# A gated attention and FFN block: the order of every engine fixed in the kernel by a model of engine times

## The chip, the cores and the metric

The kernel runs on one core of one Trainium2 chip. The metric is the device time of one execution in microseconds (us). All runs quoted here are in the fast state (the record calls a run slow when it takes over 1.5% longer than the fastest of the same kernel), and medians are given with the range of the runs. The granted clock is the share of TensorE's full clock that the profile shows as granted. A "ratio" is the mean time of one kernel's fast runs over the mean of the other kernel's fast runs of the same rounds, so it is not quite the ratio of the two medians that stand beside it. The kernel before was timed again in each batch of runs (medians 803.54 to 805.38), and every ratio is taken within its own batch. The kernel after was timed in the first comparison only. So the differences to it in us, given below, are between medians of different batches, and they are uncertain by some 2 us, as the medians of the kernel before show. The three batches of experiments also ran on three different chips.

Engine names in the profile: PE is the matmul engine (TensorE), PEld its weight load, DVE is VectorE, ACT is ScalarE, POOL is GpSimd, and SP issues most of the DMAs. "L182" is line 182 of that kernel's file; the two kernels and the experiments have different line numbers.

## The reference, cut to what matters

```python
x = A_x                                         # 2048 tokens x 1024
g = sigmoid((x * gate_w).sum(-1, keepdims=True))
a = windowed_attention(x @ wqkv) @ wo           # 32 heads, window of 8 keys, dilation 2
b = (gelu(x @ w_gate) * (x @ w_up)) @ w_down    # 1024 -> 3584 -> 1024
return g * a + (1 - g) * b                      # bf16
```

## The kernel before

The tokens are cut into four chunks of 512, numbered c. FFN runs twice, each time over two chunks ("FFN 0" for chunks 0 and 1, "FFN 1" for 2 and 3). Each chunk needs: projections to q, k, v (PE); a gate (PE matmul, then a VectorE transpose `zt`, a clip `zc`, a ScalarE exp `ez`); attention (nearly all VectorE); its share of FFN (PE, with ScalarE and VectorE moving each product out of PSUM, the memory into which PE writes); and the down stage, which multiplies the FFN result by `w_down` and the attention result by `wo` together.

FFN and the down stage use a scheme of seven block products in place of eight. It needs sums and differences of blocks of the operands, called form sums here: of `w_down` and `wo` (prepared once, `prep_forms`), of the FFN weights (in FFN 0), of x and of the FFN result. These form sums are VectorE work too.

Here are the parts that the argument touches:

```python
def gate(c):
    pz = bank("pz")
    for kt in range(KT):
        nc.tensor.matmul(pz[:], lhsT=gcol[:, kt:kt + 1].to_broadcast([P, P]), rhs=xT(c, kt), ...)
    zt = work.tile([P, SC], F32, tag="u2", bufs=2, name="zt")
    nc.vector.transpose(out=zt[:], in_=pz[:])                               # L182
    nc.vector.tensor_scalar(out=zc[:], in0=<column of zt>, ...)             # L184, clip
    nc.scalar.activation(out=ez[:], in_=zc[:], func=ACT.Exp)                # L187
    ...

def prep_forms(i0):
    ...
    nc.vector.tensor_tensor(out=fo[:, 0], in0=b12, in1=b11, op=ALU.subtract)       # L297
    nc.vector.tensor_tensor(out=fo[:, 1], in0=b22, in1=fo[:, 0], op=ALU.subtract)  # L298
    ...                                                                            # L299, L300

def ffn(sup):
    for i in range(FT + 2):                        # FT = 28
        if i < FT:
            A[f] = bank("pA")
            mm(A[f], "A11", B11, f, True)          # L343: the first product
            Bk[f] = bank("pB")
            with hp():
                nc.scalar.copy(out=Bk[f][:], in_=A[f][:])   # L363: the "seed", PE adds onto it
    ...

# main program (hp() marks high priority for the scheduler)
qkv_outer(0, 0, wq)
prep_forms(0); prep_forms(2)
qkv_one(0, 1, wk)
qkv_one(0, 2, wv)
with hp():
    gate(0)
for i0 in range(4, NPREP, 2):
    prep_load(i0)
    prep_forms(i0)
attention(0)
halo(1)
qkv_one(1, 0, wq); qkv_one(1, 1, wk); qkv_one(1, 2, wv)
with hp():
    gate(1)
attention(1)
for sup in range(NSUP):
    c0 = 2 * sup
    x_forms()
    ffn(sup)
    if sup + 1 < NSUP:
        load_xT(c0 + 2)                            # 8 transposing loads of x on SP
    down(c0)
    ...                                            # qkv, gate, attention, load_xT, down of the next chunks
```

The program order gives only priorities. A scheduler in the framework decides, when the kernel is built, in which order each engine gets its instructions. What follows from such an order is shown by the traces below: an engine stands idle for the instruction at the head of its queue while work behind it is ready.

Of the kernel before, what the change touches and what calls it, by code (L numbers as in the profile page):

```python
# [12 lines left out]
AP = bass.AP  # L13
# [10 lines left out]
HP = 100000  # L24
# [3 lines left out]
def _win_ap(src: bass.AP, dims):  # L28
    return AP(src.tensor, src.offset, [list(src.ap[0])] + [list(d) for d in dims])


@with_exitstack
def kernel(
# [38 lines left out]

    consts = ctx.enter_context(tc.tile_pool(name="consts", bufs=1))
    persist = ctx.enter_context(tc.tile_pool(name="persist", bufs=1))
    ring = ctx.enter_context(tc.tile_pool(name="ring", bufs=5))
    work = ctx.enter_context(tc.tile_pool(name="work", bufs=2))
    small = ctx.enter_context(tc.tile_pool(name="small", bufs=1))
    psum = ctx.enter_context(tc.tile_pool(name="psum", bufs=8, space=bass.MemoryType.PSUM))
# [10 lines left out]
    vT = [persist.tile([P, NT, HALO + SC], BF16, name=f"vT{i}") for i in range(2)]  # L89
    gcol = consts.tile([P, KT], BF16)  # L90
    ident = consts.tile([P, P], BF16)

# [6 lines left out]
    def ring_tile():  # L99
        return ring.tile([P, RT], BF16, tag="ring", name="rg")  # L100

    def bank(name):
        return psum.tile([P, SC], F32, tag="mm", name=name)

    def hp():
        return tc.high_priority(offset=HP)

# [4 lines left out]
    pwarm = bank("pwarm")  # L112
    for i in range(5):
        nc.tensor.matmul(pwarm[:], lhsT=warm[:, 0:P], rhs=warm, start=True, stop=True)
# [3 lines left out]
    for i in range(1):  # L118
        nc.vector.memset(kT[0][:, :, 0:HALO], 0.0)
        nc.vector.memset(vT[0][:, :, 0:HALO], 0.0)  # L120

    def qkv_load(which, pieces, vbuf=False):
        tiles = []
        for hf in range(2):
            if vbuf:
                wv = hT[:, hf * KH:(hf + 1) * KH, 0:NT, :].rearrange("p k f n -> p k (f n)")
            else:
                wv = ring_tile()[:].rearrange("p (k n) -> p k n", k=KH)
            for (k0, k1) in pieces:
                r0 = (hf * KH + k0) * P  # L130
                nc.sync.dma_start(out=wv[:, k0:k1, :],
                                  in_=A_wqkv[r0:r0 + (k1 - k0) * P, which * D:(which + 1) * D]
                                  .rearrange("(k p) n -> p k n", p=P))
            tiles.append(wv)
        return tiles

    def qkv_mm(ps, tiles, t, kt, c):
        lhsT = _win_ap(tiles[kt // KH][:, kt % KH, t:t + 1], [[NT, P]])
        nc.tensor.matmul(ps[:], lhsT=lhsT, rhs=xT(c, kt), start=(kt == 0), stop=(kt == KT - 1))  # L139

    def halo(c):
        cc = c % 2
        if c > 0:
            pc = 1 - cc
            nc.scalar.copy(out=kT[cc][:, :, 0:HALO], in_=kT[pc][:, :, SC:SC + HALO])
            nc.scalar.copy(out=vT[cc][:, :, 0:HALO], in_=vT[pc][:, :, SC:SC + HALO])
# [5 lines left out]
    def qkv_outer(c, which, tiles):  # L152
        banks = [bank("ps") for t in range(NT)]
        for kt in range(KT):
            for t in range(NT):
                qkv_mm(banks[t], tiles, t, kt, c)
        for t in range(NT):
            if t % 2 == 0:
                nc.scalar.copy(out=qkv_dst(c, which, t), in_=banks[t][:])
            else:  # L160
                nc.vector.tensor_copy(out=qkv_dst(c, which, t), in_=banks[t][:])

    def qkv_one(c, which, tiles):
        for t in range(NT):
            ps = bank("ps")
            for kt in range(KT):
                qkv_mm(ps, tiles, t, kt, c)
            nc.scalar.copy(out=qkv_dst(c, which, t), in_=ps[:])

    def qkv(c):  # L170
        halo(c)
        for which in range(3):
            qkv_one(c, which, qkv_load(which, [(0, KH)]))

    gates = {}

    def gate(c):
        pz = bank("pz")
        for kt in range(KT):
            nc.tensor.matmul(pz[:], lhsT=gcol[:, kt:kt + 1].to_broadcast([P, P]), rhs=xT(c, kt), start=(kt == 0), stop=(kt == KT - 1))  # L180
        zt = work.tile([P, SC], F32, tag="u2", bufs=2, name="zt")
        nc.vector.transpose(out=zt[:], in_=pz[:])  # L182
        zc = small.tile([P, SC // 32], F32, tag="zc", name="zc")
        nc.vector.tensor_scalar(out=zc[:], in0=zt[:].rearrange("p (b j) -> p b j", j=32)[:, :, 0],  # L184
                                scalar1=ZMAX, scalar2=-ZMAX, op0=ALU.min, op1=ALU.max)
        ez = small.tile([P, SC // 32], F32, tag="ez", bufs=2, name="ez")
        nc.scalar.activation(out=ez[:], in_=zc[:], func=ACT.Exp)  # L187
        og = small.tile([P, SC // 32], F32, tag="og", name="og")
        nc.vector.tensor_scalar(out=og[:], in0=ez[:], scalar1=1.0, scalar2=1.0, op0=ALU.mult, op1=ALU.add)
        nc.vector.reciprocal(out=og[:], in_=og[:])  # L190
        omg = small.tile([P, NST], F32, tag="omg", bufs=3, name="omg")
        for q in range(4):
            nc.vector.tensor_copy(out=omg[32 * q:32 * (q + 1), :],
                                  in_=og[32 * q:32 * (q + 1), :].rearrange("p (j q) -> p j q", q=4)[:, :, q])
        gates[c] = (ez, omg)

    def attention(c):
        cc = c % 2
        q_, k_, v_ = qo[cc], kT[cc], vT[cc]
        ez = gates[c][0]  # L200
        for a in range(SC // AC):
            a0 = a * AC
            acc = work.tile([P, NWIN, AC], BF16, tag="b0", bufs=1, name="acc")
            for t in range(NT):
                q_b = q_[:, t, a0:a0 + AC].rearrange("p (o s) -> p o s", o=1).to_broadcast([P, NWIN, AC])
                k_w = _win_ap(k_[:, t, HALO + a0:HALO + a0 + AC], [[-DIL, NWIN], [1, AC]])
                if t == 0:
                    nc.vector.tensor_tensor(out=acc[:], in0=q_b, in1=k_w, op=ALU.mult)
                else:
                    prod = work.tile([P, NWIN, AC], BF16, tag="b1", bufs=1, name="prod")  # L210
                    nc.vector.tensor_tensor(out=prod[:], in0=q_b, in1=k_w, op=ALU.mult)  # L211
                    nc.vector.tensor_tensor(out=acc[:], in0=acc[:], in1=prod[:], op=ALU.add)  # L212
            accT = work.tile([P, CW, DL], BF16, tag="b1", bufs=1, name="accT")
            nc.vector.transpose(out=accT[:].rearrange("p c d -> p (c d)"), in_=acc[:].rearrange("p w s -> p (w s)"))
            nxt = work.tile([P, CW, 2], BF16, tag="s4", bufs=1, name="nxt")
            nc.vector.tensor_tensor(out=nxt[:], in0=accT[:, :, 0:2], in1=accT[:, :, 2:4], op=ALU.add)
            lsb = work.tile([P, NWIN, CB], F32, tag="b1", bufs=1, name="lsb")
            nc.vector.tensor_tensor(out=lsb[:].rearrange("p w c -> p (w c)"), in0=nxt[:, :, 0], in1=nxt[:, :, 1],
                                    op=ALU.add)
            if c == 0 and a == 0:  # L220
                for q in range(4):
                    for w in range(1, NWIN):
                        nc.vector.memset(lsb[32 * q:32 * q + DIL * w, w, 0:HQ], NEG)
            m4 = small.tile([P, 4, CB], F32, tag="m4", name="m4")
            nc.vector.tensor_tensor(out=m4[:], in0=lsb[:, 0:4, :], in1=lsb[:, 4:8, :], op=ALU.max)
            nc.vector.tensor_tensor(out=m4[:, 0:2, :], in0=m4[:, 0:2, :], in1=m4[:, 2:4, :], op=ALU.max)
            nc.vector.tensor_tensor(out=m4[:, 0, :], in0=m4[:, 0, :], in1=m4[:, 1, :], op=ALU.max)
            m_b = m4[:, 0:1, :].to_broadcast([P, NWIN, CB])
            nc.vector.tensor_tensor(out=lsb[:], in0=lsb[:], in1=m_b, op=ALU.subtract)
            nc.scalar.activation(out=lsb[:], in_=lsb[:], func=ACT.Exp, scale=scale)  # L230
            d4 = small.tile([P, 4, CB], F32, tag="m4", name="d4")
            nc.vector.tensor_tensor(out=d4[:], in0=lsb[:, 0:4, :], in1=lsb[:, 4:8, :], op=ALU.add)
            nc.vector.tensor_tensor(out=d4[:, 0:2, :], in0=d4[:, 0:2, :], in1=d4[:, 2:4, :], op=ALU.add)
# [12 lines left out]
            for t in range(0, NT, 2):  # L246
                pall = work.tile([P, 2, NWIN, AC], BF16, tag="b0", bufs=1, name="pall")
                for u in range(2):
                    v_w = _win_ap(v_[:, t + u, HALO + a0:HALO + a0 + AC], [[-DIL, NWIN], [1, AC]])
                    nc.vector.tensor_tensor(out=pall[:, u], in0=ab[:], in1=v_w, op=ALU.mult)  # L250
# [147 lines left out]
    def down(c):  # L398
# [21 lines left out]
        def quarter(j, kh):  # L420
            return (hq(j, kh), oq(j, kh))
# [194 lines left out]
```

## Time and profile before

| | before |
|---|---|
| device time, median (range) | 805.86 us (804.89 to 805.9), 3 of the 4 runs of the result below |
| span of the profiled run, granted clock | 802.9 us, 0.972 |
| matmuls of 512 columns in the program | 3376 |
| their pitch (from the start of one to the start of the next) at full clock | 4 in 0.863 us, so 0.2158 us each: 729 us |
| start before the first projection, tail after the last product | 8 and 4 us (the prediction booked 5) |
| floor from these | 740 us (742 in the prediction) |

The pitch agrees with the Trainium skill, "TensorE: Matmul & The Clock Gate", Part 1, which gives 215.7 ns. The first lines below are from the profile page of the kernel before: the busy table, three rows of the picture in 40 slices (a digit is the busy share of a slice in tenths; one slice is 20 us; PEclk is the granted clock in tenths) and the chain of work that ended last, as shares of the span.

```profile
PE 743.0 (93%) x3345; PEld 370.6 (46%) x3413; DVE 599.7 (75%) x811; ACT 302.6 (38%) x511; POOL 48.4 (6%) x81
...
PE   8992967999999995999999999599989999999998
...
DVE  2457999988999895999989989979989533631201
...
PEclk9996997999999997999999999799999999999999
...
PE 58%; DVE 22%; DMA 8%; issue 5%; ACT 3%; SPq 1%; POOL 1%; ACTq 0%; DVEq 0%; POOLq 0%
```

PE is the limit nearly everywhere, with dips in four places: around 60 to 80, 110, 305 and 510 us. In each the granted clock drops as well. PE's own waits, the three largest (total, times, longest, in us), name the dips:

```profile
PE pA L343 <- ACT pB L363: 20.3, 5, 9.7
PE ps L139 <- DVE zt L182: 14.2, 1, 14.2
PE qA L466 <- DMA rg<-in_B_w_down_dram: 9.2, 2, 8.6
```

The 14.2 us is the gate of chunk 0, at 63 to 78 us. The 20.3 us are seeds before FFN 0 (9.4) and FFN 1 (9.7) and three short ones. The 8.6 us is a wait at 307 us for down weights: in SP's timeline transposing loads of x stand ahead of them.

What kept `zt` away for so long stands in VectorE's timeline (start, duration, instruction, and in brackets the idle time before it and what ended that):

```profile
61.17 0.69 DVE L297 TENSOR_TENSOR hT<-hT 128x1024 bf16<-128x1024 bf16 x1 [2.35 <-DMA hT<-in_B_w_down_dram]
...
66.98 0.69 DVE L299 TENSOR_TENSOR hT<-hT 128x1024 bf16<-128x1024 bf16 x1 [1.58 <-DMA hT<-in_B_w_down_dram]
...
72.51 0.69 DVE L299 TENSOR_TENSOR hT<-hT 128x1024 bf16<-128x1024 bf16 x1 [1.89 <-DMA hT<-in_A_wo_dram]
...
74.91 0.69 DVE L297 TENSOR_TENSOR hT<-hT 128x1024 bf16<-128x1024 bf16 x1 [1.10 <-DMA hT<-in_A_wo_dram]
...
76.12 1.22 DVE L211 TENSOR_TENSOR prod<-qo_81,kT_83 128x2048 bf16<-128x2048 bf16 x1
77.25 0.71 DVE L182 STREAM_TRANSPOSE zt<-pz 128x512 f32<-128x512 f32 x1
```

The gate matmul had ended at 52 us. VectorE came to `zt` at 77.25, because preparation sums that waited for their loads stood before it in the queue. VectorE was idle for each of them, while attention work of chunk 0 stood behind it. Summed over the run, the first line below (from the groups: busy us, mean ns, then idle time just before the group and what ended it) has 21.8 us of such idleness. The second is from the windows view and has the busy time of VectorE and PE from 20 to 120 us:

```profile
L297 DVE TENSOR_TENSOR hT<-hT 128x1024 bf16<-128x1024 bf16 x9 | 6.2, 691 | 21.8 <-DMA hT<-in_B_w_down_dram 20.7 <-DMA hT<-in_A_wo_dram 1.1
```

Gate 1 is late. Its matmul ended at 111.6 us, and `zt` follows ten attention steps of chunk 0; these are the last step and `zt`:

```profile
120.40 1.22 DVE L250 TENSOR_TENSOR pall<-ab,vT_85 128x2048 bf16<-128x2048 bf16 x1
121.53 0.71 DVE L182 STREAM_TRANSPOSE zt<-pz 128x512 f32<-128x512 f32 x1
```

### The profile page before, as it was taken

Reading aid. Unit: us, or ns where it says so; the run is one execution under the profiler, and the core shown is the slowest. Engines: PE = TensorE matmul, PEld = TensorE weight load, DVE = VectorE, ACT = ScalarE, POOL = GpSimd, SP = SyncE. Lnnn points to the kernel's source line nnn. Section 1 sums busy time; section 2 is a strip of 40 time slices with the busy share of each in tenths; the row PEclk is TensorE's granted clock in tenths of the full one; section 3 lists DMA queues with packets and bytes.
Section 4 is the critical chain, followed back from the end, with each engine's and each line's share of the span. In section 5 each row is a group of like instructions: output and inputs, shape, how many; then the busy total and the mean of one; then the engine's idle time right before and its main releaser. Section 6 shows DMA issues by size and latency. Waiting matters only on the chain.

```text
span 802.9 us, 9027 instructions
## 1 busy us (share of the span) xinstructions
PE 743.0 (93%) x3345; PEld 370.6 (46%) x3413; DVE 599.7 (75%) x811; ACT 302.6 (38%) x511; POOL 48.4 (6%) x81
## 2 busy tenths in 40 slices
PE   8992967999999995999999999599989999999998
PEld 5661643444444442446654466244434444444443
DVE  2457999988999895999989989979989533631201
ACT  1320244566545740113331043275575555310110
POOL 2144100000000000010000000000000000001000
PEclk9996997999999997999999999799999999999999
DMA  9999530546546379897558973325444454789984
GB/s 309 308 343 375 165 124 2 180 142 202 163 152 210 106 228 235 292 313 255 169 183 295 325 267 107 93 91 169 133 158 145 131 182 146 235 290 324 324 316 174
DMA packets 128523, 167.84 MB, mean 209 GB/s; under 512 B 17888, under 2 KB 105952, under 8 KB 124896
## 3 DMA queue, kind: packets, MB, share of 16 engines
q1 hardware_dynamic: 122112, 139.48, 54.0%
q0 software_dynamic: 6080, 27.27, 8.8%
q8 instruction: 26, 0.43, 0.2%
q10 hardware_dynamic: 288, 0.52, 0.2%
q14 instruction: 17, 0.14, 0.1%
HBM read 135.79 MB, written 28.31 MB: 204 GB/s over the span
## 4 chain that ended last, share of the span: by engine, by line
PE 58%; DVE 22%; DMA 8%; issue 5%; ACT 3%; SPq 1%; POOL 1%; ACTq 0%; DVEq 0%; POOLq 0%
PE ps L139 12%; PE qB L466 10%; PE pB L343 9%; PE qD L466 8%; PE qA L466 8%; PE pA L343 6%; PE pD L343 6%; DVE acc L212 3%; DVE prod L211 3%; DVE pall L250 2%; DMA hT<-in_B_w_down_dram 2%; DMA rg<-in_A_wqkv_dram 2%; DMA rg<-in_B_w_down_dram 2%; DVE hT L382 2%; DVE hT L369 2%
## 5 line engine op out<-in xcount | busy, mean ns | idle before, releaser
L343 PEld LDWEIGHTS <-rg 128*128 128x128 bf16 x1568 | 154.3, 98 | 215.6 <-issue 35.1
L139 PE MATMUL ps<-xr,rg 128*128 128x512 bf16 x626 | 140.9, 383 | 16.7 <-DVE zt L182 14.2
L343 PE MATMUL pA<-xr,rg 128*128 128x512 bf16 x439 | 115.3, 383 | 21.0 <-ACT pB L363 20.3
L139 PEld LDWEIGHTS <-rg 128*128 128x128 bf16 x640 | 91.9, 144 | 65.0 <-issue 17.2
L343 PE MATMUL pB<-tf,rg 128*128 128x512 bf16 x439 | 115.4, 383 | 1.7 <-DVE hT L382 0.8
L466 PEld LDWEIGHTS <-hT 128*128 128x128 bf16 x672 | 66.1, 99 | 90.4 <-DMA rg<-in_B_w_down_dram 9.1
L466 PE MATMUL qB<-rg,hT 128*128 128x512 bf16 x330 | 76.1, 379 | 0.3
L212 DVE TENSOR_TENSOR acc<-acc,prod 128x2048 bf16<-128x2048 bf16 x56 | 68.3, 1220 | 1.0
L466 PE MATMUL qA<-rg,hT 128*128 128x512 bf16 x220 | 53.3, 390 | 9.4 <-DMA rg<-in_B_w_down_dram 9.2
L343 PE MATMUL pD<-xr,rg 128*128 128x512 bf16 x220 | 57.8, 383 | 3.0 <-ACT m_4599 L377 1.3
L343 PE MATMUL pB<-xr,rg 128*128 128x512 bf16 x218 | 56.8, 379 | 0.4 <-ACT u_2264 L392 0.2
L343 PE MATMUL pD<-tf,rg 128*128 128x512 bf16 x220 | 57.0, 379 | 0.2
L369 DVE TENSOR_TENSOR hT<-hT,gl 128x1024 bf16<-128x1024 bf16 x56 | 38.3, 684 | 18.0 <-ACT hT L368 17.8
L388 ACT ACTIVATE gl<-pA 128x512 bf16<-128x512 f32 x56 | 33.5, 599 | 30.6 <-PE pA L343 27.1
L363 ACT COPY pB<-pA 128x512 f32<-128x512 f32 x56 | 32.3, 576 | 30.8 <-PE pA L343 30.8
L470 POOL DMA_DIRECT2D out_dram<-ost x24 | 13.0, 542 | 448.9 <-ACT ost L492 341.1
L250 DVE TENSOR_TENSOR pall<-ab,vT_86 128x2048 bf16<-128x2048 bf16 x32 | 38.7, 1216 | 0.0
L250 DVE TENSOR_TENSOR pall<-ab,vT_85 128x2048 bf16<-128x2048 bf16 x32 | 38.6, 1217 | 0.0
L211 DVE TENSOR_TENSOR prod<-qo_81,kT_83 128x2048 bf16<-128x2048 bf16 x28 | 34.2, 1222 | 1.1
L211 DVE TENSOR_TENSOR prod<-qo_82,kT_84 128x2048 bf16<-128x2048 bf16 x28 | 34.1, 1219 | 0.8
L368 ACT CAST hT<-pB 128x512 bf16<-128x512 f32 x56 | 32.2, 575 | 5.2 <-PE pB L343 4.8
L510 DVE SCALAR_TENSOR_TENSOR ost<-qB,omg,m5d 128x512 bf16<-128x512 f32 x8 | 6.0, 747 | 35.0 <-issue 28.7
(548 smaller groups left out, 841.8 us busy)
## 6 DMA issues: line engine op xcount, KB each, us to landing
rg<-dforms SPq DMA_DIRECT2D x32, 896.0 KB, 6.6
rg<-in_B_w_down_dram SPq DMA_DIRECT2D x24, 896.0 KB, 6.7
rg<-in_A_wqkv_dram SPq DMA_DIRECT2D x14, 1024.0 KB, 7.9
rg<-in_B_w_gate_dram SPq DMA_DIRECT2D x28, 512.0 KB, 3.9
fforms<-rg POOLq DMA_DIRECT2D x14, 1024.0 KB, 6.4
rg<-fforms SPq DMA_DIRECT2D x14, 1024.0 KB, 4.8
rg<-oforms SPq DMA_DIRECT2D x16, 512.0 KB, 3.5
hT<-in_B_w_down_dram SPq DMA_DIRECT2D x28, 256.0 KB, 6.6
```

The source lines that it names most:

```text
L139: nc.tensor.matmul(ps[:], lhsT=lhsT, rhs=xT(c, kt), start=(kt == 0), stop=(kt == KT - 1))
L211: nc.vector.tensor_tensor(out=prod[:], in0=q_b, in1=k_w, op=ALU.mult)
L212: nc.vector.tensor_tensor(out=acc[:], in0=acc[:], in1=prod[:], op=ALU.add)
L250: nc.vector.tensor_tensor(out=pall[:, u], in0=ab[:], in1=v_w, op=ALU.mult)
L343: nc.tensor.matmul(bk[:], lhsT=w, rhs=rhs[:, k, :], start=(start and k == 0), stop=(k == KH - 1), skip_group_check=True)
L363: nc.scalar.copy(out=Bk[f][:], in_=A[f][:])
L368: nc.scalar.copy(out=hs(f, 0), in_=v3(Bk[f][:]))
L369: nc.vector.tensor_tensor(out=hT[:, :, f, :], in0=hT[:, :, f, :], in1=gl[f][:].rearrange("p (j s) -> p j s", s=P), op=ALU.mult)
L382: nc.vector.tensor_tensor(out=hs(f, 1), in0=v3(Bk[f][:]), in1=v3(m5[f][:]), op=ALU.add)
L388: nc.scalar.activation(out=gl[f][:, SC:2 * SC], in_=A[f][:], func=ACT.Gelu_apprx_tanh)
L466: nc.tensor.matmul(bk[:], lhsT=l, rhs=w[i], start=(start and i == 0), stop=(i == n - 1), skip_group_check=True)
L470: eng.dma_start(out=o2[s0 + j * P:s0 + (j + 1) * P, nh * NW:(nh + 1) * NW], in_=ost)
```

## The change

Its intent: don't leave the order to the scheduler. Every operation becomes an `Op` with an engine, a modelled cost and the operations that it needs. Six streams (the matmul stages, loads, weight form sums, x form sums, preparation sums, attention) are Python generators. At each step the stream whose next operation can start earliest by the model (plus a small fixed bias of its stream) gets its turn. Each instruction is then chained to the one before it on its engine, so that the scheduler can't move it. Buffers (PSUM banks, the ring of weight slots, attention's scratch) are handed out by the same model.

```diff
+class Weave:
+    def _start(self, op):
+        ...
+        t = self.clk[op.eng]
+        for d in deps:
+            t = max(t, d.end + self.LAT + (op.lag if d.eng != op.eng else 0.0))
+        return t
+
+    def _emit(self, op, t):
+        ...                                     # advance the engine's modelled clock, call op.fn()
+            prev = self.last.get(eng)
+            if prev is not None:
+                self.tc.add_manual_dep(ins, prev, ..., reason="engine order")
+            self.last[eng] = ins.name
+
+    def run(self, streams):
+        while live:
+            ...                                 # the stream with the smallest t + bias goes next
+            self._emit(s[2], t)
@@
+    MM = 0.2128                                 # modelled us of one matmul
@@
+    def tt(n, f32=False):                       # modelled us of a VectorE tensor_tensor
+        return 0.07 + n / (960.0 if f32 else 1920.0)
@@ the transposing loads of x go two by two behind down weights
-        if sup + 1 < NSUP:
-            load_xT(c0 + 2)
-        down(c0)
+        yield from load_down(c0, load_x(c0 + 2, [("ffn", sup)]) if more else ())
@@ the gate
-        with hp():
-            gate(0)
+        e = dve(0.63, lambda: nc.vector.transpose(out=zt[:], in_=banks[i][:]), [o])
+        ...
+        e = act(0.1, lambda: nc.scalar.activation(out=ez[:], in_=zc[:], func=ACT.Exp), [e], table="exp", lag=1.0, ...)
@@ end of the program
+    w.run([(0.0, main()), (0.0, loads()), (0.1, wforms()), (0.1, x_forms()), (0.15, preps()), (0.3, attention())])
... (the bodies of ffn, down, attention and the loads are rewritten as generators; the expansion copy
     `ex` and the transpose behind it in attention are cut into halves; the arithmetic stays)
```

The matmuls are the same, and so is nearly all VectorE and ScalarE work.

## The prediction

> **What bounds it now.** TensorE. The table of engines has it 93% busy, but the floor is its pitch: in the timeline 4 FFN matmuls of 512 columns take 0.863 us, 0.2158 each (the Trainium skill, "TensorE: Matmul & The Clock Gate", Part 1, gives 215.7 ns warm; the trace agrees). The kernel has 3376: 729 us. With 8 us before the first projection and 5 after the last: about 742. The span is 802.9, so some 60 us are stalls. The list of PE's waits and the timeline place them:
> - 63-78 us: 14.2 us on the VectorE transpose of gate(0), which stood behind attention and form sums waiting for loads;
> - 114-124 and 507-517: 9.4 and 9.7 us before FFN 0 and FFN 1. The releaser shown is a ScalarE seed, but in the chain of waits that stood behind VectorE's gate transpose (121.5, 514.5), again behind attention;
> - 306-315: 8.6 us for the first down weights, queued on SP behind 16 transposing loads of x.
> A granted clock of 0.5-0.7 follows each, some 2 us more (the same page says an idle array falls to half clock). The rest: table loads in FFN 1 (2 us), and FFN iterations of 6.2 us where 28 matmuls need 6.04.
>
> **What changes.** Same matmuls, almost the same VectorE and ScalarE work (ex and its transpose are halved: 2 us less blocking). Order, fixed buffers and the SP queue change. From the built order: gate transposes stand where their matmul should end; the form sums of x come before gate(0); weight forms of block 0 before the last preparation loads; down weights before the x transposes, which go two by two into the down stage.
>
> **Budget.** I summed the measured VectorE pitches (2048 elements 1.14 us, 1.26 when it reads what the one before wrote; 1024: 0.60; PSUM operand 0.62; transpose 2.22) along the new order. Gate(1) falls at 95 us, as in PE's own count, so FFN 0 should start at 98-101 rather than 124. In FFN 0 VectorE needs 5.94 us per iteration, PE 6.04: nearly a tie, and as gelu stands before the next seed on ScalarE, PE follows VectorE with little slack. I take 6.2, as before: end about 273. Down(0), projections, down(1), projections: 54.4+43+54.4+43 us, plus 3 for each down stage (its DMA share is already 0.86-0.92, and 8 x transposes come on top): 474. From gate(2) to gate(3) VectorE needs about 103 us against PE's 97.5: 3 us of stall before FFN 1. FFN 1 172, down(2) and down(3) 109, tail 5: span about 762, device time 764.
>
> So 33 us of gate stalls, 9 of the down start and 5 of cold clock lie on the critical path and go; some 10 come back as coupling of PE to VectorE and DMA pressure.
>
> **Prediction:** 764 us, 8 in 10 between 751 and 784. Faster by over 2%: 0.92; within 2%: 0.06; slower: 0.02.
>
> **What would show it.** PE's waits on gate transposes and seeds under 3 us each; FFN 0 starting at 98-101; no gap at the first down stage; granted clock above 0.98 on average; FFN iterations 6.1-6.3 us, with short PE waits on ScalarE seeds released through VectorE; down(0), down(1) 54-58 us at a DMA share over 0.9.
>
> **What would make it wrong.** The order comes from a model whose VectorE ops are cheaper (1.14, never 1.26): if VectorE lags, an in-order ScalarE hands each lag to PE, and FFN iterations grow to 6.5 us (+16). Late preparation loads could stop VectorE before gate(0). Transposing loads could starve down weights by over 5 us per stage. Better: FFN iterations at 6.04, then 752.

## More of the kernel before

VectorE is under-used in the first four slices and then close to full until about 640 us.

```profile
20.00:120.00 100.00, 78.36 (x349) 49.85 (x355) 72.14 (x123) 26.95 (x49) 24.34 (x34) 0.92 0.81 264
```

The columns of a window are: bounds and length; busy time and count of PE, PEld, DVE, ACT and POOL; granted clock, DMA share, GB/s. VectorE worked 72.14 of these 100 us and PE 78.36.

## The result and the profile after

| | before | after |
|---|---|---|
| device time, median (range), 4 runs each | 805.38 us (803.16 to 805.9) | 766.98 us (766.42 to 767.78) |
| ratio of fast runs, 95% interval | | 0.9529, 0.9509 to 0.9549 |
| span of the profiled run | 802.9 us | 764.6 us |
| granted clock | 0.972 | 0.990 |

The page of the kernel after, the same rows:

```profile
PE 738.1 (97%) x3345; PEld 370.3 (48%) x3413; DVE 606.3 (79%) x827; ACT 303.4 (40%) x519; POOL 48.3 (6%) x81
...
PE   8999989999999999999799997999999999999997
...
DVE  2799999999999799989999989989998933603201
...
PEclk9999999999999999999899999899999999999999
...
PE 79%; DVE 10%; DMA 5%; ACT 4%; issue 2%; SPq 0%; ACTq 0%; DVEq 0%
```

Busy time hardly moved on any engine (VectorE even has 6.6 us more). What went is PE's idleness: the dips at 60 to 80, 110 and 305 us are gone, smaller ones are left at 375 and 480 us. VectorE is nearly full from the second slice on. PE's largest waits are now:

```profile
PE ps_90 L656 <- ACT ps_94 L683: 6.3, 1, 6.3
PE ps_94 L801 <- ACT ps_92 L834: 4.0, 1, 4.0
PE ps_96 L656 <- DVE hT L721: 1.8, 1, 1.8
```

The group that answers to L297 is L407 in this kernel, and its idleness fell from 21.8 to 6.5 us:

```profile
L407 DVE TENSOR_TENSOR hT<-hT 128x1024 bf16<-128x1024 bf16 x9 | 6.1, 681 | 6.5 <-DMA hT<-in_B_w_down_dram 6.5
```

In the windows, VectorE does 92.91 us of work from 20 to 120 us in place of 72.14, PE 96.98 in place of 78.36. From 120 to 470 us VectorE is busy 334.39 of 350 us, 96%:

```profile
20.00:120.00 100.00, 96.98 (x442) 58.85 (x450) 92.91 (x158) 41.25 (x73) 24.84 (x35) 1.00 0.88 280
120.00:470.00 350.00, 342.59 (x1549) 172.71 (x1580) 334.39 (x424) 140.25 (x240) 14.53 (x27) 0.99 0.68 215
```

By stages, read from PE's timeline in both traces (us from the start of the span):

| | before | after | gained so far |
|---|---|---|---|
| FFN 0 runs without a stall over 2 us from | 124.2 | 98.4 | 26 |
| FFN 0 ends | 301.2 | 269.4 | 32 |
| down stage of chunk 0 ends | 364.3 | 323.7 | 41 |
| first product of FFN 1 | 505.6 | 471.4 | 34 |
| FFN 1 runs again after its stall from | 517.1 | 479.6 | 38 |
| end | 802.9 | 764.6 | 38 |

So 26 us come from the start of FFN 0, that is mainly from the gates of chunks 0 and 1. FFN 0 adds 6 and the first down stage 9 (before, nine matmuls of that stage, 2 us, ran inside FFN 0; counted with their stage it is 4 and 11). About 6 us are given back before FFN 1. They lie in the down stage of chunk 1: it takes 61.3 us from 366.9 to 428.2, against 54.4 before (408.05 to 462.44). This is how it happens; the lines are from the timeline of all engines of the kernel after (L535 is now `zt`, L545 `ez`, L834 the seed of the down stage):

```profile
374.32 0.71 DVE L535 STREAM_TRANSPOSE zt<-ps_90 128x512 f32<-128x512 f32 x1
...
375.27 0.22 ACT L545 ACTIVATE ez<-zc 128x16 f32<-128x16 f32 x1 [9.30 <-DVE zc L539]
...
377.64 0.63 ACT L608 ACTIVATE rb<-rb 128x512 f32<-128x512 f32 x1 [2.15 <-DVE rb L605]
...
378.17 0.58 ACT L834 COPY ps_92<-ps_94 128x512 f32<-128x512 f32 x1
...
378.81 1.01 PE L801 MATMUL ps_94<-rg_88,hT 128*128 128x512 bf16 x2 [3.96 <-ACT ps_92 L834]
```

PE ended the matmul of gate 2 at 367. VectorE reached `zt` only at 374.3. ScalarE had `ez` at the head of its queue and stood still for 9.30 us, then waited 2.15 us for the attention's exp, while the seed that PE needed stood third. The Trainium skill ("TensorE: Matmul & The Clock Gate", opening table) calls the queues of ScalarE and VectorE strict FIFO, and this is that, with its price: 3.96 us of PE. The same happens at 480 us: `ez` waits 8.37 us, and PE 6.29 us for the seed behind it. After that stall eight matmuls take 3.36 us (479.58 to 482.94), 0.42 each, so half clock (granted clock 0.50). That agrees with the same page, Part 1, which has the array at half rate for about 3.4 us after an idle window. After the stall at 375 us it was longer: fourteen matmuls take 5.83 us (378.81 to 384.64), 0.42 each.

### The profile page after: what moved, and what is told of

Read it like the earlier page. It is cut to its first block, busy times and chain, and to the rows that moved or that the text cites. A ratio compares the mean times of both kernels' runs of the same rounds, so it can differ in the third digit from the quotient of the medians.

```text
span 764.6 us, 9068 instructions
## 1 busy us (share of the span) xinstructions
PE 738.1 (97%) x3345; PEld 370.3 (48%) x3413; DVE 606.3 (79%) x827; ACT 303.4 (40%) x519; POOL 48.3 (6%) x81
## 4 chain that ended last, share of the span: by engine, by line
PE 79%; DVE 10%; DMA 5%; ACT 4%; issue 2%; SPq 0%; ACTq 0%; DVEq 0%
PE ps_90 L656 5%; PE ps_91 L656 5%; PE ps_96 L656 5%; PE ps_92 L656 5%; PE ps_94 L656 5%; PE ps_89 L656 5%; PE ps_93 L656 5%; PE ps_92 L801 5%; PE ps_95 L656 4%; PE ps_89 L801 4%; PE ps_93 L801 4%; PE ps_91 L801 4%; PE ps_96 L801 4%; PE ps_94 L801 3%; PE ps_90 L801 3%; PE ps_95 L801 3%
## 5 line engine op out<-in xcount | busy, mean ns | idle before, releaser
L801 PEld LDWEIGHTS <-hT 128*128 128x128 bf16 x672 | 66.4, 99 | 85.3 <-issue 7.5
L589 DVE TENSOR_TENSOR ra<-ra,rb 128x2048 bf16<-128x2048 bf16 x56 | 68.5, 1223 | 1.3
L656 PEld LDWEIGHTS <-rg_84 128*128 128x128 bf16 x448 | 43.8, 98 | 52.9
L656 PEld LDWEIGHTS <-rg_86 128*128 128x128 bf16 x344 | 33.8, 98 | 47.3 <-issue 7.1
L656 PEld LDWEIGHTS <-rg_85 128*128 128x128 bf16 x344 | 34.0, 99 | 43.8 <-issue 4.2
L639 DVE TENSOR_TENSOR rc<-ra 128x2048 bf16<-128x2048 bf16 x32 | 39.1, 1222 | 0.8
L637 DVE TENSOR_TENSOR ra<-rb,vT_83 128x2048 bf16<-128x2048 bf16 x32 | 38.1, 1218 | 0.1
L637 DVE TENSOR_TENSOR ra<-rb,vT_82 128x2048 bf16<-128x2048 bf16 x32 | 38.1, 1219 | 0.1
L588 DVE TENSOR_TENSOR rb<-qo_78,kT_80 128x2048 bf16<-128x2048 bf16 x28 | 34.2, 1222 | 2.0 <-ACT kT_80 L494 0.5
L656 PEld LDWEIGHTS <-rg_88 128*128 128x128 bf16 x216 | 21.1, 98 | 29.3 <-issue 4.2
L588 DVE TENSOR_TENSOR rb<-qo_79,kT_81 128x2048 bf16<-128x2048 bf16 x28 | 34.2, 1220 | 0.7
L656 PEld LDWEIGHTS <-rg_87 128*128 128x128 bf16 x216 | 21.1, 98 | 27.4 <-issue 2.2
L474 PEld LDWEIGHTS <-rg_86 128*128 128x128 bf16 x160 | 23.0, 144 | 11.6
L772 DVE TENSOR_TENSOR hT<-hT 128x1792 bf16<-128x1792 bf16 x16 | 17.4, 1086 | 8.7 <-PE ps_94 L801 3.8
L416 POOL DMA_DIRECT2D dforms<-hT x28 | 20.3, 725 | 49.9 <-DVE hT L407 47.4
L474 PEld LDWEIGHTS <-rg_84 128*128 128x128 bf16 x128 | 18.5, 144 | 9.9 <-issue 0.7
L474 PEld LDWEIGHTS <-rg_87 128*128 128x128 bf16 x128 | 18.2, 143 | 9.9 <-DMA rg_87<-in_A_wqkv_dram 0.8
L474 PEld LDWEIGHTS <-rg_85 128*128 128x128 bf16 x128 | 18.4, 143 | 9.3
L474 PEld LDWEIGHTS <-hT 128*128 128x128 bf16 x128 | 18.4, 143 | 9.3
L640 DVE TENSOR_TENSOR rc<-rc 128x1024 bf16<-128x1024 bf16 x32 | 22.0, 689 | 0.8
```

Of the source, the lines that this page charges most:

```text
L416: lambda f=f: nc.gpsimd.dma_start(out=dd[:, f, r0:r0 + n, :], in_=fo[:, f]), [last],
L474: nc.tensor.matmul(banks[bk][:], lhsT=lhsT, rhs=xT(c, kt), start=(kt == 0), stop=(kt == KT - 1))
L588: yield dve(tt(n), lambda q_b=q_b, k_w=k_w: V(out=prod, in0=q_b, in1=k_w, op=ALU.mult), d, lag=0.5)
L589: yield dve(tt(n), lambda: V(out=acc, in0=acc, in1=prod, op=ALU.add))
L637: yield dve(tt(n), lambda u=u, v_w=v_w: V(out=pall[:, u], in0=ab, in1=v_w, op=ALU.mult), [("qkv", c, 2, t + u)] + halo_v, lag=0.5)
L639: yield dve(tt(n), lambda: V(out=s4, in0=pall[:, :, 0:4], in1=pall[:, :, 4:8], op=ALU.add))
```

## The experiments

Ten kernels were run, in three batches. Each was timed in three rounds against the kernel before. All outputs are right.

### Is it the fixed order, or the rewriting? (nochain)

The kernel after, with the chain left out. The operations are still emitted in the modelled order, but the scheduler may move them.

```diff
-            if prev is not None:
+            if prev is not None and False:
```

> The changed kernel, emitted in the same order, but without the chain that ties each instruction to the one before it on its engine: the scheduler may reorder again. In the built order the gate(1) transpose then has 9.5 us more VectorE work before it, and ten of the sixteen x transposes stand in a row before the weights of the second down product. If the chain itself is worth something: 771 to 779 us, with a DMA wait of 4 to 8 us early in down(0) and FFN 0 starting 2 to 6 us later than at 95. If the emission order and the fixed buffers do it all and the chain adds nothing: within 2 us of 767.

Measured: 787.84 us (786.91 to 788.51), ratio to before 0.9813 [0.9797, 0.9829]. Both expectations missed; the chain is worth more than either thought. Of the signs, the DMA wait of 4 to 8 us came, but FFN 0 was held until 111.7 us, far more than 2 to 6 us later. PE's waits:

```profile
PE ps L656 <- ACT m L705: 19.1, 9, 13.1
PE ps L801 <- DMA rg<-in_B_w_down_dram: 6.9, 1, 6.9
PE ps L656 <- ACT u L740: 4.7, 1, 4.7
```

The stalls before FFN 0 (13.1), before the second product of the first down stage (6.9) and before FFN 1 (4.7) came back; the one on the gate of chunk 0 did not. Of the 38 us between the two kernels, about 21 hang on the chain, and the order of emission with the new buffers gives the other 17 (23 and 15 if the two ratios are compared).

### Is it when VectorE gets to the gates? (lategate)

The kernel after, where the model is told that `zt` becomes ready later, so that it is placed late in VectorE's order.

```diff
-        e = dve(0.63, lambda: nc.vector.transpose(out=zt[:], in_=banks[i][:]), [o])
+        e = dve(0.63, lambda: nc.vector.transpose(out=zt[:], in_=banks[i][:]), [o], lag=(25.0, 12.0, 0.0, 10.0)[c])
```

> The changed kernel with the four gate transposes made to come 25, 12, 0 and 10 us later in the modelled order (18 us more VectorE work before gate(1), 10 more between gate(2) and gate(3)); all else as it was. If the place of the gate transposes was what cost the kernel before its stalls: FFN 0 starts its second product 14 to 19 us later than after, and the time is 780 to 790. If the gain came from filling VectorE early and from the load order, and the gates hardly matter: under 771.

Measured: 796.64 us (795.88 to 797.37), ratio 0.992 [0.9905, 0.9935]. The theory holds, and its size was set too low: most of the gain is gone, with the stalls where they had been (72, 121 and 508 us):

```profile
PE ps L656 <- ACT ps L683: 33.0, 5, 16.6
PE ps L474 <- DVE zt L535: 8.9, 1, 8.9
```

This shows that late gates are enough to lose most of the gain. VectorE did 88.81 us of work from 20 to 120 us in this run, nearly the 92.91 of the kernel after, so filling VectorE early does not bring the gain while the gates stand late. The run does not show what made the gates late in the kernel before.

### What made the gates late before? (gatefirst, preplate)

First, the kernel before with each gate emitted ahead of its chunk's projections, so that its matmul ends much earlier.

```diff
     qkv_outer(0, 0, wq)
+    with hp():
+        gate(0)
     prep_forms(0)
@@
     qkv_one(0, 2, wv)
-    with hp():
-        gate(0)
... (the same for gates 1, 2 and 3)
```

> The kernel before with one change: each gate is computed ahead of the projections of its chunk, so that a late transpose on VectorE has some 40 us before a matmul needs its bank or its exponential. If the three gate stalls (33 us and some cold clock) are a cost of their own: 768 to 780, with FFN 0 starting near 100 and FFN 1 without its 9.7 us wait. If they were only where a VectorE shortage showed (it idled for loads in the first 60 us), the loss comes back at other VectorE ops: 790 or more.

Measured: 804.56 us (803.68 to 805.82), ratio 1.002 [1.0004, 1.0036]. The rival holds: nothing is gained. `zt` of gate 0 now runs at 32 us, but the gate matmul of chunk 1 has moved forward too, and PE waits 17.5 us for its `zt`, which VectorE reaches at 81 us, again behind form sums that wait for `wo`. The form sums' idleness is as before (22.4 us):

```profile
PE ps L139 <- DVE zt L182: 18.8, 2, 17.5
PE pB L343 <- DVE hT L382: 11.0, 4, 8.7
```

```profile
L297 DVE TENSOR_TENSOR hT<-hT 128x1024 bf16<-128x1024 bf16 x9 | 6.2, 691 | 22.4 <-DMA hT<-in_B_w_down_dram 19.9 <-DMA hT<-in_A_wo_dram 2.2
```

So the moment at which PE delivers the gate is not the point; VectorE has less work done than it could have. The second kernel leaves the gates alone and changes what may fill VectorE's waits:

```diff
+    attention(0)
     for i0 in range(4, NPREP, 2):
         prep_load(i0)
         prep_forms(i0)
-    attention(0)
```

> The kernel before with one edit: attention of chunk 0 is written ahead of the remaining preparation loads and their form sums, so the scheduler may put attention, not sums that wait for loads, at the head of VectorE's queue. Theory (form sums waiting for their loads at the head of VectorE's in-order queue make gate(0) and gate(1) late): VectorE is busy about 15 of 20 us in 20-40 us as in the kernel after, the stall of PE on the transpose of gate(0) (14.2 us) and most of the 9.4 us before FFN 0 go, with the cold clock behind them; the stalls at 306 and 507 us stay: 780 to 790 us. Rival (it is the amount of VectorE work, or the later half of the preparation, that makes FFN 0 start late): the work only changes places and FFN 0 still starts after 117 us: 797 to 806 us.

Measured: 794.13 us (793.4 to 795.55), ratio 0.9874 [0.9854, 0.9895], between the two expectations. The filling came later than expected: VectorE worked 9.61 us from 20 to 40 us (8.96 before; about 15 were expected), but 18.51 us from 40 to 60 us (10.77 before). PE's waits, and the group of form sums:

```profile
PE pA L343 <- ACT pB L363: 24.5, 5, 16.9
PE qA L466 <- DMA rg<-in_B_w_down_dram: 7.8, 1, 7.8
...
PE ps L139 <- DVE zt L182: 1.9, 1, 1.9
```

```profile
L297 DVE TENSOR_TENSOR hT<-hT 128x1024 bf16<-128x1024 bf16 x9 | 6.2, 685 | 15.5 <-DMA hT<-in_B_w_down_dram 15.3
```

The stall on gate 0 went from 14.2 to 1.9 us, so the waiting form sums were its cause. But FFN 0 starts at 115.5 rather than 124.2, and its stall grew from 9.4 to 16.9 us. In VectorE's timeline a weight form sum of FFN 0 then waits 5.49 us for its load (until 96.9), and fifteen attention steps of chunk 0 stand ahead of `zt` of gate 1, which comes at 112.8 although its matmul had ended at about 95. So the two gates are late for different reasons: gate 0 behind sums that wait for loads, gate 1 behind attention work that happened to be put ahead of it, as in the kernel before. One edit to the priorities mends the first and lets PE wait longer at the second. The order of the kernel after deals with both: `zt` of gate 1 runs at 96.5, with steps of chunk 0's attention before and after it.

### Is the place of the transposing loads worth the down stall? (xfirst)

The kernel after, with all eight transposing loads of the next x before the first down weights. (In the kernel before, fourteen such loads stood before the weights of the second product.)

```diff
-            yield from load_down(c0, load_x(c0 + 2, [("ffn", sup)]) if more else ())
+            if more:
+                yield from load_x(c0 + 2, [("ffn", sup)])
+            yield from load_down(c0)
```

> The changed kernel with all eight x transposes of chunk 2 put on the SP queue ahead of the weights of down(0), as the kernel before had them. If the place in the queue was the cause of the stall at 306 us before: PE waits 6 to 10 us for weights at the start of down(0), the granted clock drops there, and the time is 775 to 780. If not: within 2 us of 767.

Measured: 781.31 us (780.89 to 782.62), ratio 0.9732 [0.9717, 0.9746]. The theory holds and is slightly low: 14.3 us more than the kernel after. The first wait is 12.3 us and ends at 285 us; a second of 6.0 us follows and ends at 328 us:

```profile
PE ps L803 <- DMA rg<-in_B_w_down_dram: 12.3, 1, 12.3
...
PE ps L803 <- ACT u2d L825: 6.0, 1, 6.0
```

Only the first is a wait for weights. At the second, PE waits for the copy `u2d`, which stands on ScalarE behind an exp of attention that itself waited 10.48 us for VectorE. So this part of the loss is VectorE's lag again, in an order that the model had laid out anew. In the kernel after, with two transposing loads behind each product's weights, the down stage of chunk 0 takes 54.4 us, which is 252 matmuls at 0.2158: PE's own pace, at a DMA share of 1.07 as the profile counts it.

### Where do the remaining stalls come from? (calib, ezlate, calibez)

Theory: the model is a little wrong. It takes 1.137 us for a VectorE operation of 2048 elements and 0.2128 us for a matmul. The trace of the kernel after has both pitches of VectorE in three lines:

```profile
351.82 1.22 DVE L586 TENSOR_TENSOR ra<-qo_78,kT_80 128x2048 bf16<-128x2048 bf16 x1
352.96 1.22 DVE L588 TENSOR_TENSOR rb<-qo_78,kT_80 128x2048 bf16<-128x2048 bf16 x1
354.21 1.23 DVE L589 TENSOR_TENSOR ra<-ra,rb 128x2048 bf16<-128x2048 bf16 x1
```

From L586 to L588, which need nothing of each other, it is 1.14 us; from L588 to L589, which reads what L588 wrote, 1.25. In the chains of attention nearly every operation either reads what the one before wrote or overwrites what the one before read, and the latter took 1.24 to 1.33 us (L589 to L588). By gate 3 `zt` comes 6.5 us after its matmul has ended (477.9 against 471.4), and the model has placed `zt` and `ez` by its own clock. The kernel `calib` corrects only these two numbers:

```diff
-    MM = 0.2128
+    MM = 0.2158
-        return 0.07 + n / (960.0 if f32 else 1920.0)
+        return 0.07 + n / (960.0 if f32 else 1920.0) + (0.12 if n >= NWIN * AC else 0.0)
```

> The changed kernel with its model of times corrected from the trace: 0.12 us more for each VectorE operation of 2048 elements (1.26 measured where it follows the one it reads) and 0.2158 instead of 0.2128 us per matmul. If the two late stalls (4.0 us at 375, 6.3 us at 473, each with cold clock after it) come from VectorE lagging the model: both fall under 2 us and the time is 756 to 761. If they have another cause: 765 to 768.

Measured: 759.67 us (758.92 to 760.33), ratio 0.9445 [0.942, 0.9469]. The theory holds: 7.3 us from two constants. The stall at 375 is gone and the waits at the start of FFN 1 are 1.1 and 1.5 us. As the whole order is laid out anew, three other waits of 2.1 to 3.8 us appear, at 99, 107 and 273 us.

The rival cure is to take `ez` out of ScalarE's way. `ezlate` moves the gate's exp and what follows it behind the first ScalarE copy that PE needs, leaving the model as it was:

```diff
         gates[c] = (ez, omg)
+        tails[c] = gate_tail(c, e, zc, ez, omg)     # exp, 1 + exp, reciprocal, omg
+        if c == 0:
+            yield from tails[c]
@@ in ffn, behind the first m5 copy
+                if i == 0:
+                    yield from tails[2 * sup + 1]
@@ in the down stage of chunk 1, behind its second seed
+                    if g == 1 and c == 1:
+                        yield from tails[2]
```

> The changed kernel with only the gate's exponential (and what follows from it) put behind the first bank seeds on ScalarE, so that a late gate transpose no longer holds those seeds; the model is not corrected. If PE stalls because ScalarE, in order, hands VectorE's lag on: the wait at 375 goes, the one at 473 shrinks to 2 to 5 us as the next operation that needs VectorE meets the same lag: 758 to 764. If the lag only moves to the next operation in full: 766 to 768.

Measured: 765.59 us (764.18 to 767.31), ratio 0.9519 [0.9492, 0.9547]: between the two expectations, and no clear difference from the kernel after. The wait at 375 went as expected, but at 480 the lag only moved on. `zt` is as late as before (477.7 us), and PE now waits 8.1 us for a later ScalarE copy at 481 us, which stands behind that same exp (9.10 us of idle ScalarE before it) and a table load:

```profile
PE ps L663 <- ACT u L749: 8.1, 1, 8.1
```

Both together:

> Both of the above: corrected model and late exponential. Expected to be the fastest: 753 to 758, no PE wait over 2 us after the start, granted clock 0.995 or more.

Measured: **751.48 us (750.88 to 753.2), ratio 0.9349 [0.9318, 0.9379]**, a little below the expected range, 15.5 us below the kernel after, and with a span (749.5 us) within 10 us of the floor. No wait of PE is over 1.8 us:

```profile
PE ps L663 <- ACT ps L690: 3.3, 3, 1.3
PE ps L663 <- DVE hT L730: 3.3, 2, 1.7
```

Once the model is right, the later exp is worth 8.2 us; with the wrong model it is worth nothing measurable. The two effects are not additive. This is the best version of the study.

### Is filling VectorE's early waits worth its time? (attlate, calibattl)

Both hold back chunk 0's attention until the form sums of the sixth pair of preparation loads are stored (the step with the key `("preps", 10)`; the second expectation calls it the tenth sum), once in the kernel after and once in the best version.

```diff
-            d = [("qkv", c, 0, t), ("qkv", c, 1, t)] + halo_k
+            d = [("qkv", c, 0, t), ("qkv", c, 1, t)] + halo_k + ([("preps", 10)] if c == 0 and a == 0 else [])
```

> The changed kernel with attention(0) held back until the form sums of the sixth load pair are stored (about 17 us of VectorE work leave the first 60 us, where it then idles for loads as in the kernel before); the model knows of it and places the gates accordingly. If a wrong place of the few operations that PE waits for is what costs, and an idle VectorE early does not: 766 to 773. If the early filling of VectorE by itself carries the gain: 778 or more.

Measured: 773.25 us (771.36 to 773.94), ratio 0.961 [0.9583, 0.9637], 6.3 us above the kernel after and just above the range of the first expectation. The loss shows only from 419 us on, with a wait of 9.4 us before FFN 1.

> The kernel after with the corrected model times and the later exp of the gate (751.5 us as measured), and in addition the attention of chunk 0 held back until the tenth preparation sum is done, so that VectorE again waits idly for loads early on. Theory A (filling VectorE's early waits with attention is worth its full time, as the work comes back behind the gates): 756 to 762 us, with VectorE busy under 11 of 20 us in 20-40 us and new PE stalls near 100 us or before 480 us. Theory B (with right model times the order leaves VectorE enough slack by gate(1) and gate(3) to absorb it): 750 to 754 us.

Measured: 767.64 us (766.9 to 770.63), ratio 0.9551 [0.9521, 0.9582], 16.2 us above the best version. Theory A holds, and even its range was too low. VectorE's busy time from 20 to 120 us is 69.19 us, against 91.21 in the best version (first fence the best version, second this one):

```profile
20.00:120.00 100.00, 98.53 (x456) 59.32 (x455) 91.21 (x157) 42.64 (x76) 24.84 (x35) 1.00 0.90 290
```

```profile
20.00:120.00 100.00, 99.47 (x455) 60.20 (x463) 69.19 (x129) 42.03 (x75) 24.85 (x35) 1.00 0.90 290
```

In this window PE loses nothing: 99.47 us busy. The 22 us of VectorE work that were left undone come back as 16 us of PE stalls and cold clock, nearly all between 371 and 482 us, some 250 us after the window's end. The largest waits are before FFN 1 (6.0) and in the down stage of chunk 1 (3.4):

```profile
PE ps L663 <- ACT ps L690: 7.3, 4, 6.0
...
PE ps L810 <- DVE ost L874: 3.4, 1, 3.4
```

VectorE is 95% busy from 120 to 470 us in this run, so it can hardly catch up. In the weaker kernel the same edit cost only 6.3 us. That one had 4.0 and 6.3 us of stalls at 375 and 480 us already, and the model laid out everything afresh; that this is why the two costs differ is argued, not shown.

## Why the prediction was right

The prediction said 764 us (751 to 784); the median was 766.98. Point by point:

- **The bound and the floor: right.** PE's pitch, 0.2158 us, stood up. The floor is 740 us rather than 742, as the tail is 4 us; the best version's span is 749.5.
- **The early gate stalls, right in their size, only in part in their cause.** FFN 0 was expected at 98 to 101 and runs from 98.4 (its first product is at 95.4, then 1.1 us of stall). The prediction put the wait on gate 0 to "attention and form sums waiting for loads", and that of gate 1 to attention. `gatefirst` and `preplate` separate them: the loads' waits made gate 0 late (14.2 to 1.9 us when some of them are filled), and attention ahead in the queue, without any wait, made gate 1 late.
- **The down start: right.** 8.6 us went; `xfirst` shows that the place of the transposing loads decides it. The weights were those of the second product and not, as the prediction has it, the first.
- **"plus 3 for each down stage" for DMA: wrong in its cause, nearly right in its sum.** The first down stage runs at PE's pace with all transposing loads in it: 0 us in place of 3. The second takes 7 us more than its pace, not for DMA but for gate 2 (3.96 us of wait and the cold clock behind it).
- **"3 us of stall before FFN 1": too small.** It was 6.3 us and some 2 us of half clock. The prediction named the cause in what would make it wrong, a model with 1.14 us where 1.26 is measured, but booked too little for it. `calib` measures it: 7.3 us of device time alone, 15.5 us together with the later exp.
- **"PE's waits on gate transposes and seeds under 3 us each": wrong**, 6.3 and 4.0 us. It is the same step.
- **Granted clock above 0.98: right** (0.990). **FFN iterations 6.1 to 6.3 us: right**: FFN 0 from 98.4 to 269.4 is 6.1 us for each of 28.
- **DMA share over 0.9 in down(0) and down(1): right** (1.07 and 0.94). "54-58 us" is right for the first (54.4), wrong for the second (61.3).

So the mechanism and the sign were right, but that the total was hit within 3 us is partly luck: errors of opposite sign cancelled. FFN 0 ended 3.6 us earlier than booked, and 6 us booked for DMA did not come; the lag of VectorE cost some 7 us at gate 2, where nothing was booked, and 5 us more than booked at gate 3. The halved expansion copy ("2 us less blocking") was not tested on its own. Nor was the share of the new buffers in the 17 us that remain without the chain.

## What to carry to other kernels

Where an in-order engine is nearly as full as the bound one (here 96% for 350 us), look for its idle time long before the stall: in `calibattl` 22 us lost by VectorE at 20 to 120 us came back as stops of PE at 371 to 482 us, although that kernel had the right model and the later exp. An order fixed by a model is as good as the model: read the pitch of dependent and of independent operations from a trace and put those in, since two constants were worth 7 us and made another edit worth 8 more. Put no operation that waits for a lagging engine ahead of one that the bound engine needs, on any in-order queue, DMA issue included; but `ezlate` shows that this alone gains nothing while the order behind it is planned with wrong times.

## What the Trainium skill lacked or had wrong

- "VectorE: DVE Perf Modes", § The DRAIN you can't avoid, says that a semaphore between operations costs nothing extra, with an example of copies, and the tier table has 1224 ns for a bf16 `tensor_tensor` of 2048 elements. The duration agrees (mean 1218 to 1223 ns for attention's in the kernel after). But planning an order needs the pitch; this page has none for these operations, and no page has one for operations that depend on each other. Measured: 1.14 us to a following operation that needs nothing of it, 1.25 to 1.26 us to one that reads its result, and 1.24 to 1.33 us to one that overwrites what it reads. The 0.12 us added to the model decided 7 us here (with the matmul's constant corrected in the same run). Whether it is the semaphore that costs this time, no run shows.
- "DMA: Bandwidth & Descriptors" has no measured figure for how long a transposing load holds the issuing queue on this chip among other loads (its table of the fast path has only a decode time in cycles for "previous generations"). Here two transposing loads of 512x128 bf16 took 2.62 us on SP (1.31 each), and up to 4.37 us for two later in the same down stage, against 0.32 to 0.39 us for most plain loads of weights. Eight of them ahead of the down weights cost PE a wait of 12.3 us; two behind each product's weights cost nothing.
